# Attention with a gated feed-forward block on one core: the mixed tile's weights and h1 transposed in halves, row sums inverted after they are turned, all jobs in a new order

## The chip, the core and the metric

The kernel runs on one core of a Trainium2 chip. TensorE (PE in the profile) multiplies matrices into PSUM, VectorE (DVE), ScalarE (ACT) and GpSimd (POOL) work on tiles, SyncE (SP) issues most DMAs. The engines run side by side and wait for one another through semaphores; each takes its own instructions in the order in which they were built. The metric is the device time of one execution in microseconds.

## The reference

Queries and keys are rotated (RoPE), softmax attention runs over 8 x 8 heads of 576 positions and 64 dimensions, and the heads of a batch, side by side, feed a gated block of 512 channels. The gate is a causal convolution of five taps. All data are float32.

```python
q_rot, k_rot = rotate(q), rotate(k)                  # 8, 8, 576, 64
scores = q_rot @ k_rot.T / sqrt(64)
attn = exp(scores - max(scores)); attn = attn / (sum(attn) + 1e-9)
x = (attn @ v) with heads side by side               # 8, 576, 512
gate_pre[s] = sum over k < 5 of conv_w[k] * x[s - 4 + k]
gate = 1 / (1 + exp(-gate_pre))
out = (gate * (x @ w_val)) @ w_out
```

## The kernel before

**Pairs.** The 64 heads are worked on as 32 pairs (`p`), two heads on 128 partitions; four pairs make a batch. Loads of k and q are rotated by products with a table and a sum (`rope_mul`, `rope_add`, on GpSimd or VectorE) and split into a high and a low part (`qk_hi`, `qk_lo`).

**Scores.** 576 queries are four chunks of 128 for each head and one *mixed* tile, the last 64 queries of both heads. So a pair has nine tiles of 128 queries by 576 keys. TensorE makes each out of three products of the parts (`s_mm`, L332), VectorE takes the negative maximum (L338), ScalarE the exponential and, beside it, the row sum, into one of nine columns of `sums` (L346).

**Turning the weights.** The product with v needs keys on partitions, so TensorE transposes the exponentials against the identity into PSUM banks (`ps_t`, four of them, tag `ps_t`), and VectorE or ScalarE copies them out (`t_copy`, L427 and L429). A *key* names a group. `"0"` to `"3"` are the chunks; `halves` (L395) turns them with two instructions a block, each on 64 of the 128 rows, into two banks `a` and `b`; `pt0` and `pt1` receive them. 512 of 576 keys lie in these blocks. The last 64 keys of two chunks stand next to each other: `h0` turns those of the two earlier chunks, `h1` of the two later ones, into `ptr`. `m` is the mixed tile, 512 keys in four blocks; `hm` is 73 columns: its last 64 keys and nine columns for the row sums. `h0`, `h1`, `m` and `hm` are full 128-row transposes (`transpose`, L361).

**Row sums.** `r_inv` (L458, L459) adds 1e-9 to `sums` and writes the inverse into the nine columns behind the mixed tile, so that `hm` turns them too. `r_copy` takes the nine rows out of the bank (L472), a DMA writes them to DRAM and another reads them back spread over the partitions (`rb`). `x_norm` (L489) multiplies the product with v (`pv_mm` L438, `pv_left` L448 for the last keys) by `rb`. The last pair does it in another way.

**Gate and block.** x is split in two parts (`x_hi` on ScalarE, `x_lo` on GpSimd), four taps run on VectorE (L515), one and the tanh on ScalarE. After four pairs come the two products of the block, each value out of three products of parts (`f_mm`, L555), with `y_mul` (VectorE), `y_hi` (ScalarE) and `y_lo` (GpSimd) between them. The weights' 64-bit patterns are decoded by steps on VectorE, ScalarE and GpSimd early in the program.

**The order.** The functions only add *jobs* with what they read and write. A table written out by hand, `ORDER`, lists the jobs' numbers; a letter V, A or G behind a number picks the engine where there is a choice, and the digits after a colon pick the buffers (of four `ps_t` banks, two `ps_s`, and so on). `FILLS` names steps ahead of which TensorE turns the identity a number of times into a bank that the next transposition overwrites (L354). So every engine's order is that of the table.

## Time and profile before

| | us |
|---|---|
| median of 3 runs | 709.28 (708.91 to 709.58) |
| profiled execution | 708.45 |
| its span, first to last instruction | 706.6 |
| TensorE busy | 673.5 (95%) |
| VectorE busy | 592.5 (84%) |
| ScalarE busy | 502.7 (71%) |
| GpSimd busy | 298.9 (42%) |
| mean granted clock of TensorE | 0.986 |

A busy time is the union of an engine's instructions. Consecutive matmuls overlap, so the time that one of them costs is read from its start to the start of the next one; the row's own duration is longer. Idle time of an engine counts only where another one waits for it.

### The profile page before, as it was taken

What the parts mean: (1) busy time and instruction counts of PE and PEld (TensorE: products, weight loads), DVE (VectorE), ACT (ScalarE), POOL (GpSimd) and SP (SyncE); (2) the same over time, 40 slices, a digit from 0 to 9 for tenths busy, and PEclk for the clock granted to TensorE, in tenths of its full rate; (3) what the DMA queues carried; (4) which work ended last, traced back from release to release, by engine and by line L of the source; (5) the groups of instructions that cost most, each with busy time, mean ns of one, the idle gap of its engine ahead of it and who ended that gap; (6) DMA issues with size and microseconds to landing.
All of it is one profiled execution on the core that took longest, in us unless ns stands there. A gap on an engine that the chain in (4) does not pass through costs nothing.

```text
span 706.6 us, 17745 instructions
## 1 busy us (share of the span) xinstructions
PE 673.5 (95%) x6988; PEld 539.6 (76%) x6988; DVE 592.5 (84%) x995; ACT 502.7 (71%) x1197; POOL 298.9 (42%) x231
## 2 busy tenths in 40 slices
PE   5888988899999999999999999999999999999998
PEld 4765557668787887877888877777888787888887
DVE  4989998998899888899879988898888888887731
ACT  2677877677978776777788776777777777677622
POOL 2242333556043545463424526536436744542121
PEclk9988998999999999999999999999999999999999
DMA  6343432243442143343432325323233235310212
GB/s 226 96 154 122 119 101 65 82 118 113 137 131 84 36 151 101 94 132 94 151 100 82 112 75 148 120 86 105 88 108 92 63 118 159 102 45 19 69 36 76
DMA packets 47317, 72.63 MB, mean 103 GB/s; under 512 B 15961, under 2 KB 25730, under 8 KB 47234
## 3 DMA queue, kind: packets, MB, share of 16 engines
q1 hardware_dynamic: 46690, 70.91, 32.6%
q8 instruction: 55, 0.90, 0.5%
q10 hardware_dynamic: 544, 0.59, 0.3%
q14 instruction: 28, 0.23, 0.1%
HBM read 61.89 MB, written 9.59 MB: 101 GB/s over the span
## 4 chain that ended last, share of the span: by engine, by line
PE 74%; DVE 14%; ACT 7%; issue 2%; DMA 1%; SPq 1%; POOL 0%; DVEq 0%; ACTq 0%
PE ps_f L555 27%; PE ps_s L332 18%; PE ps_a L438 13%; PE ps_t L395 8%; PE ps_t L361 5%; DVE g L515 4%; DVE nm L338 4%; ACT p L346 3%; PE ps_a L448 3%; ACT pt L427 2%; DVE q L304 1%; PE ps_r L287 1%; DMA rb<-rd 1%; DVE y L563 1%; DVE wst L594 0%
## 5 line engine op out<-in xcount | busy, mean ns | idle before, releaser
L346 ACT ACTIVATE p<-ps_s,nm 128x576 f32<-128x576 f32 x288 | 213.1, 744 | 74.3 <-DVE nm L338 72.8
L338 DVE TENSOR_REDUCE nm<-ps_s 128x1 f32<-128x576 f32 x288 | 207.8, 750 | 41.1 <-PE ps_s L332 36.6
L332 PE MATMUL ps_s<-k,q 64*128 64x288 f32 (+1 forms) x1728 | 180.6, 312 | 11.1 <-ACT p L346 10.6
L332 PEld LDWEIGHTS ps_s<-k,q 64*128 64x128 f32 (+1 forms) x1728 | 141.6, 188 | 40.4 <-ACT p L346 24.6
L427 ACT COPY pt<-ps_t 128x512 f32<-128x512 f32 x205 | 118.1, 590 | 55.3 <-PE ps_t L395 52.7
L438 PE MATMUL ps_a<-pt,v 128*64 128x256 f32 (+1 forms) x1024 | 140.8, 415 | 2.1 <-DVE y L563 1.2
L515 DVE SCALAR_TENSOR_TENSOR g<-x,cw,g 128x576 f32<-128x576 f32 (+1 forms) x132 | 121.4, 922 | 1.4 <-ACT g L512 0.8
L555 PE MATMUL ps_f<-y,wout_hi 128*128 128x288 f32 (+2 forms) x512 | 108.1, 302 | 0.0
L438 PEld LDWEIGHTS ps_a<-pt,v 128*64 128x64 f32 x1024 | 67.4, 137 | 47.8 <-issue 5.5
L395 PEld LDWEIGHTS ps_t<-ident,p 64*128 64x128 f32 x2048 | 83.4, 141 | 24.9 <-issue 7.8
L276 POOL TENSOR_TENSOR kin<-kin,tab 128x576 f32<-128x576 f32 (+1 forms) x33 | 52.5, 1598 | 116.2 <-DMA kin<-in_k 88.4
L395 PE MATMUL ps_t<-ident,p 64*128 64x64 f32 x2048 | 94.6, 228 | 6.2 <-DVE x L489 2.3
L570 POOL TENSOR_TENSOR y<-y,y 128x288 fp32r<-128x288 f32 (+2 forms) x64 | 56.7, 894 | 80.3 <-ACT y L567 76.2
L555 PEld LDWEIGHTS ps_f<-y,wout_hi 128*128 128x128 f32 x512 | 81.7, 188 | 5.8 <-ACT pt L427 2.4
L555 PE MATMUL ps_f<-xh,wval_hi 128*128 128x288 f32 (+2 forms) x256 | 78.2, 308 | 0.2 <-ACT pt L427 0.2
L555 PE MATMUL ps_f<-xl,wval_hi 128*128 128x288 f32 (+2 forms) x256 | 76.1, 299 | 0.0
L555 PE MATMUL ps_f<-xh,wval_lo 128*128 128x288 f32 (+2 forms) x256 | 75.2, 297 | 0.0
L555 PE MATMUL ps_f<-y,wout_lo 128*128 128x288 f32 (+2 forms) x256 | 74.7, 297 | 0.0
L502 POOL TENSOR_TENSOR xl<-x,xh 128x576 fp32r<-128x576 f32 (+2 forms) x33 | 49.0, 1491 | 44.3 <-ACT xh L496 44.3
L276 POOL TENSOR_TENSOR qin<-qin,tab 128x640 f32<-128x640 f32 (+1 forms) x32 | 51.8, 1628 | 37.0 <-DMA qin<-in_q 17.9
L429 DVE COPY pt<-ps_t 128x512 f32<-128x512 f32 x83 | 55.7, 678 | 6.6 <-PE ps_t L395 6.2
L346 ACT ACTIVATION_READ_ACCUMULATOR p<-ps_s,nm 128x1 f32 x288 | 57.6, 200 | 0.0
(87 smaller groups left out, 896.7 us busy)
## 6 DMA issues: line engine op xcount, KB each, us to landing
kin<-in_k SPq DMA_DIRECT2D x31, 576.0 KB, 3.8
qin<-in_q SPq DMA_DIRECT2D x31, 512.0 KB, 3.9
v<-in_v SPq DMA_DIRECT2D x32, 320.0 KB, 3.8
out_t<-o SPq DMA_DIRECT2D x56, 144.0 KB, 2.2
rb<-rd SPq DMA_DIRECT2D x31, 144.0 KB, 3.4
rb<-rd SPq DMA_DIRECT2D x31, 128.0 KB, 3.8
wst<-in_w_val SPq DMA_DIRECT2D x4, 512.0 KB
wst<-in_w_out SPq DMA_DIRECT2D x8, 256.0 KB, 3.1
```

Source lines behind the costliest of these rows:

```text
L276: eng.tensor_tensor(out=t[:, i, a:b], in0=t[:, 0 if p < RAW else i, a:b], in1=table[:, i, a:b], op=ALU.mult)
L332: T.matmul(out=tiles[h][:, half, 0:288], lhsT=st["q"][rows, x, c * 128:c * 128 + 128], rhs=st["k"][rows, y, k0:k0 + 288], start=(i == 0), ...
L338: V.tensor_reduce(out=st[f"nm{i}"], in_=st[f"s{i}"], axis=AX.XY, op=ALU.max, negate=True)
L346: A.activation(out=st[f"p{t}"][:, part].rearrange("p (b x) -> p b x", b=2), in_=st[f"s{i}"], func=AF.Exp, bias=st[f"nm{i}"], scale=1.0, ac ...
L395: T.transpose(out=st["b" + key + x][:, to:to + D], in_=f[rows, at:at + 128], identity=ident[rows, rows])
L427: A.copy(out=dst, in_=src)
L429: V.tensor_copy(out=dst, in_=src)
L438: T.matmul(out=st[f"a{g}"][HEAD[h], 0:n], lhsT=st["v"][:, j, h, :], rhs=st[f"pt{g}"][:, h * 4 + j], start=(j == 0), stop=False)
L502: G.tensor_tensor(out=st["xl"][:, a:b], in0=xs[p % 2][:, 4 + a:4 + b], in1=st["xh"][:, a:b].bitcast(F32), op=ALU.subtract)
L515: V.scalar_tensor_tensor(out=g, in0=x_sb[:, a + k:b + k], scalar=w, in1=g, op0=ALU.mult, op1=ALU.add)
L555: T.matmul(out=acc[:, 0:n], lhsT=wt[w][:, kc, ds], rhs=mv, start=(kc == 0 and i == 0), stop=(kc == NCH - 1 and i == 2))
L570: G.tensor_tensor(out=ffn[b][1][:, dc, lo:hi], in0=ffn[b, "y", dc, lo], in1=ffn[b][0][:, dc, lo:hi].bitcast(F32), op=ALU.subtract)
```

## The change

It has four parts.

1. The mixed tile's four blocks (`m`) and, except for the last pair, the two of `h1` are turned by `halves`, twelve instructions on 64 rows each, into two banks `ma` and `mb`. `h1` has no transposition of its own any more. Each bank is copied out by two jobs: 128x256 into `pt1` and 128x128 into `ptr`; before there was one of 128x512 for `m` and one of 128x256 for `h1`.
2. `r_inv` becomes one GpSimd instruction, which adds 1e-9 and writes the sums behind the mixed tile. The inverse is taken by VectorE in `r_copy`, on the turned 9x128 sums in PSUM, where ScalarE copied. The last pair stays as it was.
3. `ORDER` is a new table, with other choices of engine and of buffers. Counted in the built program, GpSimd has 31 additions of sums and 14 sums and products of the rotation more and four subtractions of k fewer; VectorE has 969 instructions instead of 995 (those it is counted by in the profile), ScalarE sixteen more, without the read-outs of its sums.
4. `FILLS` has 72 transposes of the identity in six places instead of 86 in eight.

```diff
-        if key == "m":
-            srcs = [flat(p, "m")[:, j * 128:(j + 1) * 128] for j in range(4)]
-        elif key == "hm":
+        if key == "hm":
...
     def halves(p, key):
 
         st = state[p]
-        i = order(p).index(int(key))
         for x in "ab":
             if "b" + key + x not in st:
                 st["b" + key + x] = ring("ps_t", [128, 512], F32, "ps_t", psum)
-        for h in range(2):
-            f = flat(p, f"{i // 2}{h}")
-            for j in range(4):
-                at, to = 640 * (i % 2) + j * 128, (h * 4 + j) * D
-                for x, rows in zip("ab", HEAD):
-                    T.transpose(out=st["b" + key + x][:, to:to + D], in_=f[rows, at:at + 128], identity=ident[rows, rows])
+        if key == "m":
+            srcs = [flat(p, "m")[:, j * 128:(j + 1) * 128] for j in range(4)]
+            if p < NP - 1:
+                srcs += [flat(p, f"1{h}")[:, 512:640] for h in range(2)]
+        else:
+            i = order(p).index(int(key))
+            at = 640 * (i % 2)
+            srcs = [flat(p, f"{i // 2}{h}")[:, at + j * 128:at + (j + 1) * 128] for h in range(2) for j in range(4)]
+        for k, src in enumerate(srcs):
+            for x, rows in zip("ab", HEAD):
+                T.transpose(out=st["b" + key + x][:, k * D:(k + 1) * D], in_=src[rows], identity=ident[rows, rows])
...
     def t_copy(p, key, eng):
-        bank = state[p]["b" + key]
-        if key == "m":
-            src = bank.rearrange("p (j h x) -> p j h x", j=4, h=2)
-            dst = turned(p, 1).rearrange("p (h j) x -> p j h x", h=2)[:, :, :, 256:320]
+        both = key[:2] == "h1" and p < NP - 1
+        bank = state[p]["bm" + key[2] if both else "b" + key]
+        if key[0] == "m":
+            x = "ab".index(key[1])
+            src = bank[:, 0:256].rearrange("p (j x) -> p j x", x=D)
+            dst = turned(p, 1)[:, x * 4:x * 4 + 4, 256:320]
+        elif both:
+            at = 128 + "ab".index(key[2]) * D
+            src = bank[:, 256:384].rearrange("p (h x) -> p h x", h=2)
+            dst = turned(p, "r")[:, :, at:at + D]
...
     def r_inv(p, g):
         for a, b in COLS[g]:
             r = sums[p % 2][:, a:b]
-            V.tensor_scalar(out=r, in0=r, scalar1=1e-9, scalar2=None, op0=ALU.add)
-            V.reciprocal(out=r if p == NP - 1 else state[p]["pm"][:, 1, a:b], in_=r)
+            if p == NP - 1:
+                V.tensor_scalar(out=r, in0=r, scalar1=1e-9, scalar2=None, op0=ALU.add)
+                V.reciprocal(out=r, in_=r)
+            else:
+                G.tensor_scalar(out=state[p]["pm"][:, 1, a:b], in0=r, scalar1=1e-9, scalar2=1.0, op0=ALU.add, op1=ALU.mult)
...
-            A.copy(out=st[f"rr{g}"][0:9], in_=st["bhm"][D:D + 9, 0:128])
+            V.reciprocal(out=st[f"rr{g}"][0:9], in_=st["bhm"][D:D + 9, 0:128])
...
-FILLS = {54: (25, 0, '2a', 1), 66: (16, 0, '0a', 2), 82: (11, 0, '3a', 1), 92: (8, 0, '1a', 0), 185: (6, 1, '1a', 3), 362: (8, 3, '1a', 2), 376: (8, 3, 'hm',
-         3), 463: (4, 4, '1a', 3)}
+FILLS = {50: (19, 0, '2a', 1), 63: (14, 0, 'h0', 2), 89: (7, 0, '1a', 3), 282: (9, 2, 'ma', 0), 351: (15, 3, '3a', 2), 377: (8, 3, 'ma', 3)}
```

What the new table does is seen in the built order. TensorE, pair 16, from behind its mixed scores to the next product of the block; before (a chunk's `halves` is the row x16, `h1` the row x2, `hm` the row 73x128, `m` the row x4):

```order
L555 MATMUL ps_f<-y_4300,wout_lo 128x288
L361 MATMUL ps_t<-ident,p 128x128 x2
L395 MATMUL ps_t<-ident,p 128x64 x16
L332 MATMUL ps_s<-k_72,q_74 128x288 x12
L361 MATMUL ps_t<-ident,p 73x128
L361 MATMUL ps_t<-ident,p 128x128 x4
L555 MATMUL ps_f<-xh,wval_hi 128x288
```

The same place now:

```order
L567 MATMUL ps_f<-y_4335,wout_lo 128x288
L398 MATMUL ps_t<-ident,p 128x64 x16
L333 MATMUL ps_s<-k_72,q_74 128x288 x12
L398 MATMUL ps_t<-ident,p 128x64 x12
L362 MATMUL ps_t<-ident,p 73x128
L567 MATMUL ps_f<-xh,wval_hi 128x288
```

The group x2 is gone, `m` and `h1` are the row x12, and `hm` comes after them. Ahead of this place twelve products of the block stand behind the pair's mixed scores, where there were eight.

VectorE before, at the end of the same pair's maxima (the third row is the subtraction of k for the next but one pair, the fourth and fifth are `r_inv`):

```order
L515 SCALAR_TENSOR_TENSOR g<-x_85,cw,g 128x576
L338 TENSOR_REDUCE nm<-ps_s 128x1
L307 TENSOR_TENSOR k_71<-kin,k_71 128x576
L458 TENSOR_SCALAR sums_86<-sums_86 128x9
L459 RECIPROCAL p<-sums_86 128x9
L515 SCALAR_TENSOR_TENSOR g<-x_85,cw,g 128x576
```

GpSimd now, with the same pair's addition of sums among the rotation of later pairs and the low part of an earlier x:

```order
L277 TENSOR_TENSOR qin<-qin,tab 128x640
L281 TENSOR_TENSOR kin<-kin 128x576
L514 TENSOR_TENSOR xl<-x_85,xh 128x576
L471 TENSOR_SCALAR p<-sums_86 128x9
L277 TENSOR_TENSOR kin<-kin,tab 128x576
```

And VectorE now, from the pair's last maximum to the reciprocal of its turned sums:

```order
L339 TENSOR_REDUCE nm<-ps_s 128x1
L308 TENSOR_TENSOR k_71<-kin,k_71 128x576
L527 SCALAR_TENSOR_TENSOR g<-x_85,cw,g 128x576
L438 COPY pt_5398<-ps_t 128x8x64
L527 SCALAR_TENSOR_TENSOR g<-x_85,cw,g 128x576
L339 TENSOR_REDUCE nm<-ps_s 128x1 x2
L484 RECIPROCAL rr<-ps_t 9x128
L575 SCALAR_TENSOR_TENSOR y<-g,ps_f 128x288
```

The two instructions of `r_inv` are gone from VectorE, one is in GpSimd's queue, and the reciprocal stands two maxima of the next pair further on.

280 lines of the change are left out of this document (143 added, 137 removed).

## Prediction

> **What bounds the kernel now.** I read the page's busy times and its 40 slices first. In the second fence the profile is cut into four stretches, whose columns are length, then busy time and instructions of PE, PEld, DVE, ACT and POOL, then granted clock, DMA share and GB/s.
>
> ```profile
> span 706.6 us, 17745 instructions
> PE 673.5 (95%) x6988; PEld 539.6 (76%) x6988; DVE 592.5 (84%) x995; ACT 502.7 (71%) x1197; POOL 298.9 (42%) x231
> PE   5888988899999999999999999999999999999998
> DVE  4989998998899888899879988898888888887731
> PEclk9988998999999999999999999999999999999999
> ```
>
> ```profile
> 0.00:20.00 20.00, 11.52 (x62) 8.63 (x64) 10.30 (x28) 5.90 (x15) 4.35 (x10) 1.00 0.68 221
> 20.00:145.00 125.00, 109.22 (x1092) 79.62 (x1090) 117.84 (x215) 92.81 (x220) 46.55 (x34) 0.92 0.34 104
> 145.00:690.00 545.00, 539.51 (x5745) 438.40 (x5742) 461.58 (x749) 400.06 (x953) 244.59 (x184) 1.00 0.32 99
> 690.00:706.60 16.60, 13.26 (x100) 13.00 (x98) 2.78 (x6) 3.92 (x10) 3.38 (x4) 1.00 0.23 81
> ```
>
> From 145 to 690 TensorE is idle for 5.5 of 545 us while VectorE is idle for 83: what TensorE no longer has to do there shortens the run. From 20 to 145 VectorE is busy for 94% and TensorE for 87%, partly at half clock (0.92 on the mean: 10 us of clock lost). There VectorE is the nearer bound. The first 20 us are loads and the rotation of pair 0, the last 16.6 the tail.
>
> **TensorE, the term that counts most.** Matmuls overlap at their ends, so I take what a group costs from its start to the start of the next. Here is TensorE's timeline (start, us, engine, line, operation), pair 16 in the middle, and three other places where the same groups have other neighbours:
>
> ```profile
> 335.75 0.43 PE L555 MATMUL ps_f<-y,wout_hi 128*128 128x288 f32 x2
> 336.01 0.29 PE L555 MATMUL ps_f<-y,wout_lo 128*128 128x288 f32 x1
> 336.24 0.71 PE L395 MATMUL ps_t<-ident,p 64*128 64x64 f32 x16
> ...
> 327.31 1.07 PE L332 MATMUL ps_s<-k,q 64*128 64x288 f32 x12
> 328.21 0.66 PE L395 MATMUL ps_t<-ident,p 64*128 64x64 f32 x16
> ...
> 361.79 0.38 PE L361 MATMUL ps_t<-ident,p 128*128 128x128 f32 x2
> 362.11 0.71 PE L395 MATMUL ps_t<-ident,p 64*128 64x64 f32 x16
> 362.62 1.10 PE L332 MATMUL ps_s<-k,q 64*128 64x288 f32 x12
> 363.65 0.77 PE L361 MATMUL ps_t<-ident,p 128*73 128x128 f32 x5
> 364.18 0.38 PE L555 MATMUL ps_f<-xh,wval_hi 128*128 128x288 f32 x1
> ...
> 565.28 0.33 PE L361 MATMUL ps_t<-ident,p 128*73 128x128 f32 x1
> 565.37 0.38 PE L555 MATMUL ps_f<-xh,wval_lo 128*128 128x288 f32 x1
> ```
>
> Before: two full transposes (h1) 0.32, sixteen halves 0.51, twelve score matmuls 1.03, five full ones (hm and m) 0.53: 2.39 us. The new order of pair 16 has sixteen halves, twelve scores, twelve halves, and hm alone. Sixteen halves stay 0.51. Scores that are followed by halves take 0.90 (327.31 to 328.21), 0.13 less than before full ones, and that 0.13 is now paid where the twelve halves end. Those cost 12/16 of 0.51, 0.39; hm alone 0.09 (565.28 to 565.37). The last full matmul ahead of halves costs 0.23 (336.01 to 336.24) against 0.13 for one of the two before it (0.26 from 335.75), so 0.10 more. Together 0.51 + 0.90 + 0.39 + 0.13 + 0.09 + 0.10 = 2.12, a gain of 0.27 us a pair. The count over the whole order agrees: 190 full transposes leave at 0.11 (0.53/5), 20.1 us; 380 halves come at 0.032 (0.51/16), 12.2; changes between full and divided array stay (351 and 350): 7.9 us over 32 pairs, 0.25 each. Some 25 pairs are transposed after 145 us: 25 x 0.27 = **6.8 us**. The 14 fills that go (86 to 72) stood in waits and count as nothing; without that cover they are 14 x 0.11 = 1.5 us more.
>
> The Trainium skill speaks against this, in "TensorE: Matmul & The Clock Gate", section "LDWEIGHTS (loading the stationary operand)": a weight load takes its number of columns over 1.2 GHz however few rows it fills. By that, six blocks would go from 6 x 107 = 0.64 us to twelve loads, 1.28. The trace doesn't agree for halves that alternate between the two row halves: sixteen take 0.51 us.
>
> **VectorE, ScalarE and GpSimd.** Prices from the groups by form (busy us, mean ns of one):
>
> ```profile
> L427 ACT COPY pt<-ps_t 128x512 f32<-128x512 f32 x205 | 118.1, 590 | 55.3 <-PE ps_t L395 52.7 <-PE ps_t L361 2.1
> L515 DVE SCALAR_TENSOR_TENSOR g<-x,cw,g 128x576 f32<-128x576 f32 x124 | 116.9, 943 | 0.5
> L429 DVE COPY pt<-ps_t 128x512 f32<-128x512 f32 x83 | 55.7, 678 | 6.6 <-PE ps_t L395 6.2 <-PE ps_t L361 0.3
> L427 ACT COPY pr<-ps_t 128x256 f32<-128x256 f32 x47 | 17.6, 375 | 1.1 <-PE ps_t L361 0.8
> L280 DVE TENSOR_TENSOR kin<-kin 128x576 f32<-128x576 f32 x12 | 11.5, 958 | 0.1
> L472 ACT COPY rr<-ps_t 9x128 f32<-9x128 f32 x31 | 8.0, 259 | 3.1 <-PE ps_t L361 2.4
> L459 DVE RECIPROCAL p<-sums 128x9 f32<-128x9 f32 x31 | 6.7, 216 | 1.1
> L458 DVE TENSOR_SCALAR sums<-sums 128x9 f32<-128x9 f32 x31 | 6.3, 204 | 3.6 <-ACT p L346 3.2
> L429 DVE COPY pr<-ps_t 64x128 f32<-64x128 f32 x13 | 3.6, 275 | 0.2 <-ACT rr L472 0.2
> L276 POOL TENSOR_TENSOR qin<-qin,tab 128x256 f32<-128x256 f32 x2 | 1.4, 724 | 3.1 <-ACT tab L643 3.1
> masks.py:199 POOL TENSOR_SCALAR_AFFINE_SELECT ident<-ident 128x128 f32<-128x128 f32 x1 | 0.3, 292 | 0.1
> ```
>
> Copies out of PSUM: one of 512 columns (0.59 on ScalarE) and one of 256 (0.375) become two of 256 and two of 128; those are bounded by 0.26 (the 128-column row) and 0.375, I take 0.27: 0.97 becomes 1.29 us, +0.32 a pair. Row sums: VectorE loses 0.204 + 0.216, ScalarE loses 0.259; VectorE gains a reciprocal of 9x128 out of PSUM, which no row shows. It lies between 0.216 (9 columns) and 0.678 (512 columns from PSUM); on 9 columns a reciprocal costs 12 ns more than an addition, so I take the 128-column copy, 0.28. Sum for both engines +0.32 - 0.42 - 0.26 + 0.28 = -0.08 a pair: nothing, hidden behind VectorE's 15% and ScalarE's 27% idle time after 145 us. At 0.678 VectorE would carry 31 x 0.4 = 12 us more, 2 of them early. GpSimd's addition on 9 columns lies between 0 and 0.72 (the 256-column row); near the 128-column 0.29, so 0.2.
>
> **VectorE early.** Counted in the built order ahead of the 55th maximum (pair 6's first, near 145 us) VectorE has 242 instructions before and 227 after: six additions and six reciprocals (2.5 us) against five new reciprocals (1.4); two copies of 512 columns and two small ones fewer (1.9); two rotation sums fewer (1.9); one tap fewer (0.9); two small weight steps that leave and one subtraction that comes about cancel. That is 5.8 us less. VectorE is 94% busy there, so I count 85% of it, **4.9 us**. GpSimd takes rotation work over, and with the new additions some 22 us (14 sums and products net, near 1.6 each, less four subtractions, plus 31 x 0.2). What that costs VectorE the next rows show, the first of GpSimd:
>
> ```profile
> 460.53 1.57 POOL L280 TENSOR_TENSOR qin<-qin 128x640 f32<-128x640 f32 x1
> ...
> 460.50 2.21 DVE L515 SCALAR_TENSOR_TENSOR g<-x,cw,g 128x576 f32<-128x576 f32 x1
> ...
> 362.43 0.19 ACT L346 ACTIVATION_READ_ACCUMULATOR p<-ps_s,nm 128x1 f32 x1
> ...
> 362.65 0.17 DVE L458 TENSOR_SCALAR sums<-sums 128x9 f32<-128x9 f32 x1
> 362.86 0.21 DVE L459 RECIPROCAL p<-sums 128x9 f32<-128x9 f32 x1
> 362.99 0.76 DVE L515 SCALAR_TENSOR_TENSOR g<-x,cw,g 128x576 f32<-128x576 f32 x1
> ```
>
> A tap beside a GpSimd sum took 2.21 us, another one 0.76; with the mean at 0.943, 124 taps lose 22 us beside 299 us of GpSimd work, 0.076 per us. 22 us more cost VectorE 1.7 us, mostly hidden. The Trainium skill has a rule for it ("SBUF — State Buffer", section "SBUF: two separate sides": VectorE with two SBUF inputs and GpSimd lock one port pair against each other). The trace agrees, with 2.21 against 0.76.
>
> **The new waits.** hm needs GpSimd's addition, which needs the pair's last exponential, read out at 362.62, when VectorE's addition followed within 0.03 us. In the old order hm starts 1.03 us after that, at 363.65. In the new one twelve full matmuls instead of eight (4 x 0.13) stand ahead of the halves, and from there to hm it is 0.10 + 0.51 + 0.90 + 0.39 + 0.13 = 2.03 instead of 0.32 + 0.51 + 1.03 = 1.86: hm comes 0.7 us later, 1.7 after the exponential. A free GpSimd needs 0.2 to 0.7, so this later place is the cover. If GpSimd has just begun a 1.57 us operation, it is done after 1.8, and behind hm stand all later matmuls of TensorE's order. I take one pair in four as 0.1 late, **+0.8 us**.
>
> The reciprocal of the turned sums moves from ScalarE's queue to VectorE's (in pair 16 behind two maxima), and the write and the read of the row in SP's queue follow it. Two rows say what is waited for now, one of the groups and one of TensorE's waits from 145 to 690 us:
>
> ```profile
> L489 DVE TENSOR_TENSOR x<-ps_a,rb 128x320 f32<-128x320 f32 x32 | 15.4, 483 | 13.3 <-PE ps_a L448 11.1 <-DMA rb<-rd 2.0
> ...
> PE ps_t L361 <- DVE pt L429: 0.4, 1, 0.4
> ```
>
> The row's DMA ended 2.0 us of waits in 32 pairs, TensorE's last matmul 11.1: what comes before it hides a reciprocal that is some tenths later. Without that cover it is 31 x 0.5 = 15 us on VectorE, not on TensorE. The two banks of m and h1 now wait for two copies each instead of one; TensorE waited 0.4 us for such a copy. Both count as nothing.
>
> Sum: -6.8 - 4.9 + 0.8 = -10.9. The profiled execution took 708.45 us (span 706.6 and 1.8 around it); 708.45 - 10.9 = 697.6, and its excess of the median over it, 0.83, gives **698.4 us**.
>
> **Rivals.** (a) The early gain is lost: TensorE's own waits and half clock, not VectorE, set the front. It is 87% busy there with 10 us of clock lost, which speaks for it; VectorE's 94% against it. Only 6.8 - 0.8 remain: 703.3. (b) More is gained: a third of TensorE's 15.8 idle us early closes and a third of the lost clock comes back, 5.3 + 3.4, of which VectorE's 7.2 idle us there allow some 6: 692.4. (c) Slower: GpSimd's addition stands behind an operation of 1.57 us and one tap's use of the port (0.94), so it is done 2.7 us after the exponential and hm comes 1.0 late, in twenty of the 31 pairs: 709.3 - 11.7 + 20 = 717.6. It decides from a mean wait of 0.38 us at hm (11.7/31). For it: GpSimd is 45% busy after 145 us and works in order. Against it: it is idle for the other 55%, and what stands ahead of the addition is work for later pairs. (d) No change: the same wait near 0.38, 709.3.
>
> **How the numbers follow.** The likeliest is the forecast, 0.57, with a range of its own of 694 to 702.5; (a) 0.18; (b) 0.14; (c) 0.07; (d) 0.04. The range 690.5 to 705 holds the forecast, (a) and most of (b). Under 0.2% (1.4 us) can't be told from no change here: faster 0.89, same 0.04, slower 0.07.
>
> **What would show it.** Right: full transposes down to hm and h0; the stretch after 145 us equal in idle time to before and shorter by 7 us; VectorE near 578 us; the maximum that stood at 145 us reached some 5 us earlier. Wrong: waits of TensorE for GpSimd's addition above 2 us in total, taps above 0.943 us on the mean, a reciprocal near 0.7, more half-clock time, or the front's end unmoved.

## The result, and the profile after

The changed kernel takes **729.27 us** (median of 6 runs, 726.74 to 731.54), the kernel before 709.43 beside it: a ratio of **1.0264**, 95% interval 1.0230 to 1.0297. It is 2.6% slower where 1.5% faster was forecast, and lies above the range. The profiled execution took 726.74 us.

The page of the changed kernel, busy times and slices:

```profile
span 725.0 us, 18171 instructions
PE 673.5 (93%) x7164; PEld 540.3 (75%) x7164; DVE 608.9 (84%) x969; ACT 499.3 (69%) x1213; POOL 330.5 (46%) x273
PE   5788787989999999999999999999999999999998
DVE  4899899999988889898889988889879889978641
PEclk9977799999999999999999999999999999999999
```

Its four stretches (length, then busy time and instructions of PE, PEld, DVE, ACT and POOL, granted clock, DMA share, GB/s):

```profile
0.00:20.00 20.00, 11.00 (x75) 8.44 (x76) 9.81 (x27) 6.01 (x15) 4.57 (x10) 1.00 0.59 188
20.00:145.00 125.00, 104.82 (x1057) 77.86 (x1056) 117.30 (x195) 87.57 (x216) 51.85 (x40) 0.88 0.35 109
145.00:690.00 545.00, 526.17 (x5804) 424.84 (x5803) 471.25 (x727) 397.80 (x964) 266.85 (x214) 1.00 0.32 98
690.00:725.00 35.00, 31.54 (x234) 29.17 (x232) 10.59 (x22) 7.90 (x20) 7.22 (x9) 1.00 0.17 60
```

VectorE should have come to about 578 us and stands at 608.9. TensorE's busy time is the same 673.5 us, but after 145 us it is idle for 18.8 of 545 us where it was 5.5. The early stretch has more half clock (0.88 against 0.92), not less. The groups of the changed kernel say what grew:

```profile
L527 DVE SCALAR_TENSOR_TENSOR g<-x,cw,g 128x576 f32<-128x576 f32 x124 | 119.4, 963 | 1.0 <-ACT g L524 0.4
...
L484 DVE RECIPROCAL rr<-ps_t 9x128 f32<-9x128 f32 x31 | 29.5, 952 | 2.5 <-ACT pr L436 1.3 <-PE ps_t L362 0.4
...
L471 POOL TENSOR_SCALAR p<-sums 128x9 f32<-128x9 f32 x31 | 11.3, 363 | 83.1 <-ACT p L347 78.1 <-PE ps_f L567 4.5
```

The new reciprocal takes **0.952 us**, where 0.28 was counted and 0.678 was the upper bound. Its 29.5 us, less the 6.3 and 6.7 of the old addition and reciprocal, are 16.5: as much as VectorE's busy time grew by (592.5 to 608.9); its other gains and losses (rotation, copies, taps) about cancel. The taps' mean rose by 0.020 us, 2.5 in sum. And this is how it looks on VectorE's timeline (start, us, engine, line, operation; in brackets the idle time before and what ended it) when the reciprocal stands between the two maxima of a chunk, with one row of ScalarE behind it:

```profile
537.03 0.69 DVE L438 COPY pt<-ps_t 128x512 f32<-128x512 f32 x1 [0.46 <-PE ps_t L398]
537.85 0.76 DVE L339 TENSOR_REDUCE nm<-ps_s 128x1 f32<-128x576 f32 x1
538.66 0.95 DVE L484 RECIPROCAL rr<-ps_t 9x128 f32<-9x128 f32 x1
539.64 0.76 DVE L339 TENSOR_REDUCE nm<-ps_s 128x1 f32<-128x576 f32 x1
540.32 1.89 DVE L305 SCALAR_TENSOR_TENSOR q<-qin,q 128x640 fp32r<-128x640 f32 x1
...
539.65 0.42 ACT L436 COPY pr<-ps_t 64x128 f32<-64x128 f32 x2 [0.83 <-DVE rr L484]
```

The second maximum comes 1.0 us later. ScalarE is held up too: it waits 0.83 us for the reciprocal, and behind its copies stand the exponentials of both maxima. Directly, though, the others wait little for the reciprocal: in the whole trace ScalarE 2.4 us, TensorE 3.5, GpSimd 1.6. TensorE's longest waits over the whole span, the first also for the kernel before (us in total, times, longest):

```profile
PE ps_s L333 <- ACT p L347: 18.4, 27, 1.8
PE ps_r L288 <- POOL kin L277: 8.8, 1, 8.8
```

```profile
PE ps_s L332 <- ACT p L346: 10.6, 20, 1.5
```

The one for the exponentials grew by 7.8 us; the other stands at the start of the program, and was 7.5. The start of each maximum against the same one before shows when the time is lost: the first comes 0.5 us later, the 37th 7.0, the 55th 3.1 (5 earlier was forecast), the 181st 7.4, the 217th 12.6, the last of the 288 comes 18.8 later.

### The profile page after: what moved, and what is told of

The parts are those of the page before. It is cut to its first block, busy times and chain, and to the rows that moved or that the text cites. A ratio compares the mean times of both kernels' runs of the same rounds, so it can differ in the third digit from the quotient of the medians.

```text
span 725.0 us, 18171 instructions
## 1 busy us (share of the span) xinstructions
PE 673.5 (93%) x7164; PEld 540.3 (75%) x7164; DVE 608.9 (84%) x969; ACT 499.3 (69%) x1213; POOL 330.5 (46%) x273
## 4 chain that ended last, share of the span: by engine, by line
PE 44%; DVE 9%; ACT 2%; issue 2%; ACTq 0%; DVEq 0%
PE ps_f L567 18%; PE ps_s L333 10%; PE ps_a L447 8%; PE ps_t L398 6%; DVE nm L339 3%; DVE g L527 2%; PE ps_a L457 2%; DVE rr L484 1%; ACT p L347 1%; PE ps_t L362 1%; DVE q L305 1%; DVE pt L438 0%; ACT pt L436 0%; DVE y L575 0%; ACT q L297 0%
## 5 line engine op out<-in xcount | busy, mean ns | idle before, releaser
L333 PE MATMUL ps_s<-k,q 64*128 64x288 f32 (+1 forms) x1728 | 185.1, 314 | 19.2 <-ACT p L347 18.4
L333 PEld LDWEIGHTS ps_s<-k,q 64*128 64x128 f32 (+1 forms) x1728 | 144.4, 190 | 51.8 <-ACT p L347 38.5
L436 ACT COPY pt<-ps_t 128x512 f32<-128x512 f32 (+1 forms) x236 | 125.1, 548 | 55.8 <-PE ps_t L398 55.5
L447 PE MATMUL ps_a<-pt,v 128*64 128x320 f32 (+1 forms) x1024 | 140.2, 416 | 3.8 <-ACT pt L436 1.1
L398 PE MATMUL ps_t<-ident,p 64*128 64x64 f32 x2428 | 118.3, 230 | 9.7 <-DVE pt L438 2.7
L398 PEld LDWEIGHTS ps_t<-ident,p 64*128 64x128 f32 x2428 | 103.9, 142 | 28.8 <-issue 7.1
L527 DVE SCALAR_TENSOR_TENSOR g<-x,cw,g 128x576 f32<-128x576 f32 (+2 forms) x132 | 124.1, 942 | 1.3 <-ACT g L524 0.7
L447 PEld LDWEIGHTS ps_a<-pt,v 128*64 128x64 f32 x1024 | 69.1, 138 | 49.7 <-issue 5.1
L277 POOL TENSOR_TENSOR qin<-qin,tab 128x640 f32<-128x640 f32 (+1 forms) x40 | 66.6, 1677 | 41.1 <-DMA qin<-in_q 34.7
L277 POOL TENSOR_TENSOR kin<-kin,tab 128x576 f32<-128x576 f32 (+1 forms) x31 | 51.5, 1666 | 50.6 <-DMA kin<-in_k 43.1
L438 DVE COPY pt<-ps_t 128x512 f32<-128x512 f32 (+1 forms) x84 | 51.4, 618 | 5.1 <-PE ps_t L398 4.6
```

Of the source, the lines that this page charges most:

```text
L277: eng.tensor_tensor(out=t[:, i, a:b], in0=t[:, 0 if p < RAW else i, a:b], in1=table[:, i, a:b], op=ALU.mult)
L333: T.matmul(out=tiles[h][:, half, 0:288], lhsT=st["q"][rows, x, c * 128:c * 128 + 128], rhs=st["k"][rows, y, k0:k0 + 288], start=(i == 0), ...
L398: T.transpose(out=st["b" + key + x][:, k * D:(k + 1) * D], in_=src[rows], identity=ident[rows, rows])
L436: A.copy(out=dst, in_=src)
L438: V.tensor_copy(out=dst, in_=src)
L447: T.matmul(out=st[f"a{g}"][HEAD[h], 0:n], lhsT=st["v"][:, j, h, :], rhs=st[f"pt{g}"][:, h * 4 + j], start=(j == 0), stop=False)
```

## The experiments

Each run is given as its ratio to the kernel before on the same chip, with the 95% interval; 0.1% is 0.7 us. Theory R is that the long reciprocal is the loss; O, that the new order is; G, that GpSimd's additions are. Some runs undo the change in parts, others edit the kernel before to find out what sets its time.

### A copy in the reciprocal's place

```diff
-            V.reciprocal(out=st[f"rr{g}"][0:9], in_=st["bhm"][D:D + 9, 0:128])
+            V.tensor_copy(out=st[f"rr{g}"][0:9], in_=st["bhm"][D:D + 9, 0:128])
```

> The changed kernel, with VectorE's reciprocal of the turned sums (0.95 us each in the trace) made a plain copy on VectorE (near 0.28): the inverse is left out, all else stays. Theory R (the reciprocal on 128 columns costs VectorE some 0.67 us a pair more than was counted, 21 us in all, and TensorE's waits follow from it): 698 to 706 us, TensorE idle near 35 us. Rival O (the new order itself, with GpSimd held by the additions and more half clock): 720 to 729, VectorE 20 us less busy, TensorE's waits unchanged.

711.24 us, ratio 1.0041 (1.0022 to 1.0059). Its busy times, and the row that took the reciprocal's place:

```profile
PE 669.7 (94%) x7164; PEld 538.7 (76%) x7164; DVE 588.4 (83%) x969; ACT 499.1 (70%) x1213; POOL 325.2 (46%) x273
...
L484 DVE COPY rr<-ps_t 9x128 f32<-9x128 f32 x31 | 8.8, 285 | 3.4 <-ACT pr L436 2.2 <-PE ps_t L362 0.5
```

VectorE's busy time falls by 20.5 us and the time by 2.2% (1.0264 to 1.0041), 16 us. So the reciprocal is most of the loss, although the time stays above theory R's 698 to 706 us. And with the price that the prediction had put on it (0.285 against 0.28) the change is still 0.4% slower than the kernel before, not 1.5% faster: a second error of some 14 us lies elsewhere. The profiles say where. The copy's run reaches the 55th maximum 2.2 us later than the kernel before, where 4.9 earlier was forecast; from there to the end it takes 562.6 us against 561.9, where 6.0 less was forecast. So each of the two main terms missed by some 7 us. VectorE's busy time, too, is 10 us above the 578 that were forecast.

### The sums as before, in the new order; the new sums, in the old order; the new order alone

In the first, `r_inv` and `r_copy` are those of the kernel before, at the new table's places:

```diff
-                G.tensor_scalar(out=state[p]["pm"][:, 1, a:b], in0=r, scalar1=1e-9, scalar2=1.0, op0=ALU.add, op1=ALU.mult)
+                V.tensor_scalar(out=r, in0=r, scalar1=1e-9, scalar2=None, op0=ALU.add)
+                V.reciprocal(out=state[p]["pm"][:, 1, a:b], in_=r)
...
-            V.reciprocal(out=st[f"rr{g}"][0:9], in_=st["bhm"][D:D + 9, 0:128])
+            A.copy(out=st[f"rr{g}"][0:9], in_=st["bhm"][D:D + 9, 0:128])
```

> The changed kernel with its second part undone: VectorE adds and inverts nine columns (0.20 + 0.22 us) and ScalarE copies the turned sums, each at the place that the new order gives the job. R: 698 to 706, about as the kernel with the copy. O: 720 to 729. Rival G (the addition in GpSimd's queue holds up the rotation behind it): clearly under the kernel with the copy, by 5 us or more.

724.81 us, ratio 1.0214 (1.0181 to 1.0248): in theory O's range, and rival G fails. The second is the opposite edit in the kernel before:

```diff
-            V.tensor_scalar(out=r, in0=r, scalar1=1e-9, scalar2=None, op0=ALU.add)
-            V.reciprocal(out=r if p == NP - 1 else state[p]["pm"][:, 1, a:b], in_=r)
+            if p == NP - 1:
+                V.tensor_scalar(out=r, in0=r, scalar1=1e-9, scalar2=None, op0=ALU.add)
+                V.reciprocal(out=r, in_=r)
+            else:
+                G.tensor_scalar(out=state[p]["pm"][:, 1, a:b], in0=r, scalar1=1e-9, scalar2=1.0, op0=ALU.add, op1=ALU.mult)
...
-            A.copy(out=st[f"rr{g}"][0:9], in_=st["bhm"][D:D + 9, 0:128])
+            V.reciprocal(out=st[f"rr{g}"][0:9], in_=st["bhm"][D:D + 9, 0:128])
```

> The kernel before with the second part alone: GpSimd adds, VectorE inverts the turned sums on 128 columns; order and transposes as before. R: VectorE carries 31 x (0.95 - 0.42) = 16 us more, most of it early or ahead of maxima: 716 to 728. O: 707 to 712.

731.96 us, ratio 1.0317 (1.0283 to 1.0350), and on its page:

```profile
PE 678.0 (93%) x6988; PEld 538.2 (74%) x6988; DVE 617.0 (84%) x964; ACT 494.4 (68%) x1166; POOL 312.9 (43%) x262
```

The new sums alone cost 3.2%, more than the whole change; VectorE's busy time is 24.5 us longer (16.5 by the reciprocal less what it replaces, the rest by other rows), the time 22.5. That is beyond theory R's range, and O's 707 to 712 fails. The third is the kernel before with `ORDER` as the new table has it. Where that has two copies for `ma` and `mb` (or `h1a` and `h1b`) the earlier place gets the one copy of `m` (or `h1`).

```diff
 ORDER = """
-...
+...
-FILLS = {54: (25, 0, '2a', 1), 66: (16, 0, '0a', 2), 82: (11, 0, '3a', 1), 92: (8, 0, '1a', 0), 185: (6, 1, '1a', 3), 362: (8, 3, '1a', 2), 376: (8, 3, 'hm',
-         3), 463: (4, 4, '1a', 3)}
+FILLS = {50: (19, 0, '2a', 1), 63: (14, 0, 'h0', 2), 89: (7, 0, '1a', 3), 280: (9, 2, 'm', 0), 348: (15, 3, '3a', 2), 374: (8, 3, 'm', 3)}
```

> The new order with the old transposes (m and h1 in full, at the places of the new halves, copied whole at the first of their copies' places) and the old row sums. R: the order itself is no loss, TensorE carries the 8 to 13 us of full transposes again: 706 to 715. O: 728 to 740.

722.93 us, ratio 1.0199 (1.0168 to 1.0229), between the two theories. So the new order costs 2% with full transposes and 2.1% with halves, when the sums are the old ones: at equal order the halves bring nothing that can be measured. With the new sums, though, the new order and the halves are 0.5% better than the old order (1.0264 against 1.0317, with intervals that just overlap). Its places are chosen for these sums. What this run and the one with the old sums measure is the order with jobs that it wasn't made for, and I take the copy's run as the fairer test of it. That run shows what the reciprocal costs at its place. It doesn't show that the new order would do well with any other sums: with the old ones it loses 2.1% without a 9x128 reciprocal.

### What a reciprocal costs

Behind the last instruction of the kernel before, reciprocals and other instructions of several sizes, three of each:

```diff
+        for n in (2, 9, 32, 64, 128, 256, 512):
+            for _ in range(3):
+                V.reciprocal(out=two[:, 0:n], in_=one[:, 0:n])
+        for n in (9, 128):
+            for _ in range(3):
+                V.reciprocal(out=two[0:9, 0:n], in_=one[0:9, 0:n])
+                V.reciprocal(out=two[0:9, 0:n], in_=bank[0:9, 0:n])
...
```

> The kernel before, with 57 VectorE instructions after its last one: reciprocals of 2, 9, 32, 64, 128, 256 and 512 columns on 128 partitions, three each, and of 9 and 128 columns on 9 partitions and from PSUM, beside copies, additions and products of the same sizes. Theory P (an element of a reciprocal costs VectorE about 7.4 ns whatever the partitions and the memory): 128 columns 0.95 us on 9 and on 128 partitions, from SBUF and PSUM alike, 512 columns 3.8 us, 9 columns 0.21 us; copies of 128 columns 0.2 to 0.3 us. Rival Q (the 0.952 us comes from PSUM, or from the few partitions): 128 columns of 128 partitions from SBUF below 0.5 us.

The time of this one execution (747.76 us) isn't used, only its rows (`probe` is the PSUM bank):

```profile
L809 DVE RECIPROCAL x<-x 128x512 f32<-128x512 f32 x3 | 10.1, 3353 | 0.1
...
L809 DVE RECIPROCAL x<-x 128x128 f32<-128x128 f32 x3 | 2.9, 953 | 0.1
L813 DVE RECIPROCAL x<-probe 9x128 f32<-9x128 f32 x3 | 2.8, 946 | 0.1
L812 DVE RECIPROCAL x<-x 9x128 f32<-9x128 f32 x3 | 2.8, 941 | 0.1
...
L817 DVE TENSOR_TENSOR x<-x 128x128 f32<-128x128 f32 x3 | 0.9, 292 | 0.1
...
L809 DVE RECIPROCAL x<-x 128x9 f32<-128x9 f32 x3 | 0.6, 216 | 0.1
...
L817 DVE TENSOR_TENSOR x<-x 128x9 f32<-128x9 f32 x3 | 0.5, 170 | 0.1
```

A column of a reciprocal costs (3353 - 216) / 503 = 6.2 ns, one of a product (292 - 170) / 119 = 1.0 ns. The price of a reciprocal is the same for 9 and 128 partitions and for both memories. So turning the sums from 128x9 to 9x128 makes the same 1152 inverses 0.74 us dearer. Theory P holds; only its 7.4 ns a column contained the fixed part. The Trainium skill ("VectorE: DVE Perf Modes", section "First, the fixed hardware budget") says that the reciprocal runs on iterative-divide operations with a repeat count of 8. The trace agrees that it is dear: a column costs six times as much as one of a product.

### No addition, in the old and in the new order

A row sum holds the exponential of its own maximum, about 1, so adding 1e-9 in float32 leaves it as it is. In the kernel before the addition is left out:

```diff
-            V.tensor_scalar(out=r, in0=r, scalar1=1e-9, scalar2=None, op0=ALU.add)
             V.reciprocal(out=r if p == NP - 1 else state[p]["pm"][:, 1, a:b], in_=r)
```

> The kernel before, with one thing left out: the addition of 1e-9 to the row sums. (A row sum holds the exponential of its own maximum, about 1, so in fp32 the sum stays as it is.) VectorE's 31 rows of a 128x9 addition, 5 to 6 us, go; nothing else changes. The four runs so far lie near a line in VectorE's work within one order: in the old order 650.7 us of VectorE gave 708, 672.1 us gave 732, so 1.1 us of time for each us of VectorE's work. Theory R (VectorE's work sets the time within an order): 702 to 704 us, ratio 0.991 to 0.994. Rival S (the price is the waiting at one place, where the long reciprocal stands, and a little less work elsewhere brings nothing): 707 to 709 us, within 0.2%.

706.23 us, ratio **0.9954** (0.9929 to 0.9979): the one version that is faster than both kernels beyond its interval. It lies between the two theories: only half of the expected gain came, and VectorE's busy time on its page is 592.0 us, hardly less than 592.5, although 6.3 us of additions are gone. The same group in the kernel before and in this one:

```profile
L304 DVE SCALAR_TENSOR_TENSOR q<-qin,q 128x640 fp32r<-128x640 f32 x31 | 30.4, 980 | 0.7 <-ACT q L296 0.5
```

```profile
L304 DVE SCALAR_TENSOR_TENSOR q<-qin,q 128x640 fp32r<-128x640 f32 x31 | 34.4, 1111 | 0.5 <-ACT q L296 0.5
```

In this profile 4.0 us of the gain went into the subtractions of q, each 0.13 us longer. That needn't come from the missing addition: the same 31 rows took 1.097 us on the mean in the run with more transposes below, and 1.061 in the one with the prices, which both have the addition. The new order and the halves with the same sums:

```diff
-                G.tensor_scalar(out=state[p]["pm"][:, 1, a:b], in0=r, scalar1=1e-9, scalar2=1.0, op0=ALU.add, op1=ALU.mult)
+                V.reciprocal(out=state[p]["pm"][:, 1, a:b], in_=r)
...
-            V.reciprocal(out=st[f"rr{g}"][0:9], in_=st["bhm"][D:D + 9, 0:128])
+            A.copy(out=st[f"rr{g}"][0:9], in_=st["bhm"][D:D + 9, 0:128])
```

> The changed kernel (new order, halves) with the sums inverted before they are turned, as 128x9 on VectorE (0.216 us by the kernel before), copied by ScalarE once turned, and without the addition of 1e-9; GpSimd is held up by nothing of this. The same work on the sums as in the old order without the addition, beside it in this call: the two differ by the order and the halves alone. Theory O (the new order with its halves is itself slower at equal work of VectorE, by what the line through the new order's four runs gives: 643.8 us of VectorE 711, 664.6 us 729): VectorE about 652, 716 to 719 us, 13 to 16 us above the old order without the addition. Rival R alone (only VectorE's work counts): no more than 4 us above it, 703 to 709 us.

716.56 us, ratio 1.0080 (1.0057 to 1.0104): 10.3 us above the old order with the same sums and within 1.3 us of the same VectorE busy time (593.3), within theory O's 716 to 719. And with VectorE as the one that copies the turned sums, since that place was VectorE's:

```diff
-            A.copy(out=st[f"rr{g}"][0:9], in_=st["bhm"][D:D + 9, 0:128])
+            V.tensor_copy(out=st[f"rr{g}"][0:9], in_=st["bhm"][D:D + 9, 0:128])
```

> New order and halves, the sums inverted as 128x9 on VectorE without the addition, as in the run of 716.6 us, but the turned sums copied by VectorE (0.285 us) where there ScalarE did it (0.259 us): the new order's place for this job was chosen for VectorE. There the exponential's waits at the hand-over were 51.0 us in 127 rounds, with the copy on VectorE and a GpSimd addition they were 43.1. Theory S (ScalarE's copy at a place that was not its own cost the difference): 711 to 714 us. Rival V (VectorE's work counts, 31 x 0.285 = 8.8 us more of it): 719 to 725 us.

714.95 us, ratio 1.0096 (1.0066 to 1.0127): beyond theory S's range, and no different from ScalarE's copy by these intervals. So 31 copies more on VectorE, 8.8 us, cost little or nothing at this place, where ScalarE lost 8.0 us of copies: rival V fails, and not everything that VectorE gains is paid in time.

### More fills; the old engines

The copy's kernel with 66 fills in the first pair instead of 40 (the inverse is left out here too; the kernel before has 60 there and 6 in the second pair):

```diff
-FILLS = {50: (19, 0, '2a', 1), 63: (14, 0, 'h0', 2), 89: (7, 0, '1a', 3), 282: (9, 2, 'ma', 0), 351: (15, 3, '3a', 2), 377: (8, 3, 'ma', 3)}
+FILLS = {50: (25, 0, '2a', 1), 63: (22, 0, 'h0', 2), 89: (19, 0, '1a', 3), 282: (9, 2, 'ma', 0), 351: (15, 3, '3a', 2), 377: (8, 3, 'ma', 3)}
```

> The changed kernel with a copy in the place of the 9x128 reciprocal (the inverse left out), which took 711.2 us and had 31 us of half clock, 27 of them before 125 us, where the kernel before has 20.5; and 26 more of the transposes that only keep TensorE at work in the first pair, so that it has 66 there, as many as the kernel before. Theory C (the rest of the loss is TensorE's clock, from the fewer fills): half clock falls to about 20 us, and the time to 704 to 707 us. Rival F (the front's loss is in how the new order queues VectorE's and GpSimd's work there, and the clock follows from TensorE's waiting): the fills change the time by less than 2 us, 709.5 to 713 us, whatever becomes of the clock.

710.41 us, ratio 1.0006 (0.9985 to 1.0027), 0.35% below the copy's run with intervals that just overlap, and no longer told apart from the kernel before. Early half clock (the stretches in which the trace has the granted clock at 0.5) goes from 30.7 to 27.3 us only, so theory C's condition, 20 us, isn't met, and its 704 to 707 us didn't come; a small gain by the fills isn't excluded. The other run keeps the new places but gives the 97 rope, subtraction and weight steps that had changed engine their old one, with sums as in the run of 716.56 us:

```diff
 ORDER = """
-... 13G ... 32V ...
+... 13V ... 32G ...
```

> The changed order and halves with the sums as in the run without the addition (inverted as 128x9 on VectorE, copied by ScalarE), which took 716.6 us; and for each rope, subtraction and weight step that may go to GpSimd or to VectorE, the engine that the kernel before gave it, at the new order's place. In the new order GpSimd does 14 more of these, and VectorE's 132 convolution taps took 130.9 us, against 121.7 in the old order, so that VectorE's sum is the same although it has fewer instructions. Theory G (the extra work on GpSimd slows VectorE's taps, and this is what the new order costs): taps back at 122 us, 707 to 712 us. Rival H (the places were chosen for the engines, and what the new order costs lies in where its copies and taps stand): 716 us or more.

724.16 us, ratio 1.0214 (1.0184 to 1.0243). Theory G fails, rival H holds; the taps stay slow (129.5 us in 132 of them, 130.9 with the new engines).

### What sets the time of the kernel before

Two heads' score tiles fill the two `ps_s` buffers in rounds: score matmuls, two maxima, the second exponential, the next score matmuls. First, 128 copies of 128x1 on ScalarE stand in that chain, ahead of every second exponential; then the same copies one place later, behind it:

```diff
+        bias = st[f"nm{i}"]
+        if i % 2:
+            bias = link[i // 2 % 2]
+            A.copy(out=bias, in_=st[f"nm{i}"])
```

> The kernel before, with one more ScalarE instruction for each odd score tile (128 of them): a copy of its 128x1 negated maximum to another place, and the exponential takes its bias from there, so that the copy stands between maximum and exponential. By the traces so far the two score tiles' PSUM banks go round in one chain: score matmuls, two maxima, the second exponential, the next score matmuls. After the first six pairs this chain is 511.5 of the 518.8 us in the kernel before (127 rounds of 4.03 us: 1.10 matmuls, 1.43 maxima, 0.74 exponential, and waits of 0.24, 0.31 and 0.21 at the three hand-overs). Theory T (this rotation sets the time): a link of some 0.2 us (a ScalarE read of an accumulator of 128x1 takes 0.19) makes each of 128 rounds longer, less where TensorE is late anyway: 15 to 28 us more, 724 to 737 us. Rival W (only each engine's sum of work counts, and ScalarE at 71% is no bound): 0 to 4 us more, 709 to 713 us.

```diff
+        if i % 2:
+            A.copy(out=link[i // 2 % 2], in_=st[f"nm{i}"])
```

> The same 128 copies on ScalarE, each one place later: behind the exponential, which takes its bias from the maximum itself, as in the kernel before. Theory T: ScalarE's queue is longer by the same 26 us, but the rotation isn't, apart from rounds whose next step finds ScalarE busy: 0 to 8 us more, 709 to 717 us, well under the run with the link in the chain. Rival W2 (it is ScalarE's work itself that costs, wherever it stands): as much as with the link in the chain.

In the chain: 716.37 us, ratio 1.0101 (1.0085 to 1.0118). Beside it: 707.89 us, ratio 0.9990 (0.9967 to 1.0012). The row of the first:

```profile
L350 ACT COPY link<-nm 128x1 f32<-128x1 f32 x128 | 24.4, 191 | 27.0 <-DVE nm L339 26.1 <-ACT p L351 0.2
```

Its 24.4 us cost 7 in the chain and nothing beside it. The place counts, which is theory T's mechanism, but less than half of its price came: some two thirds vanish in the chain too. Then TensorE gets more to do, three more transposes of the identity in each of 31 pairs:

```diff
+        if key == "hm" and p < NP - 1:
+            for j in (1, 2, 3):
+                T.transpose(out=bank[:, j * 128:(j + 1) * 128], in_=ident, identity=ident)
```

> The kernel before, with three more transposes of the identity in each of 31 pairs, behind the one that turns the mixed tile's last columns and in the same bank: 93 transposes at 0.11 us are 10 us more for TensorE, the opposite of what the halves save. Theory T (TensorE's work counts only where TensorE is the late one in the rotation, 0.21 us of a round of 4.03): 1 to 5 us more, 710 to 715 us. Rival B (as the prediction counted: after the front a us of TensorE's work is a us of time): 8 to 11 us more, 717 to 721 us.

715.24 us, ratio 1.0095 (1.0061 to 1.0129), between the two theories. 93 transposes, 10 us at the prediction's 0.11, cost 6.7, by the interval 4.3 to 9.1. In this run's trace the stretch from hm to the next group is 0.27 us longer (median of 25 pairs), 8.4 us for 31 pairs. So more work for TensorE does count, for most of its length and perhaps for all.

### The maxima together

Last, one edit in both orders: where another VectorE instruction stands between the two maxima of a round, the second maximum is moved ahead of it; 29 places in the kernel before without the addition, 36 in the changed kernel. One of these places (830 is the reciprocal of pair 7, 951 and 953 are the two maxima):

```diff
-818:01 ... 819A 820V 821:30 951:0 828:1 521 829A 830:1 952:2 953:3 522
+819A 820V 821:30 951:0 953:3 828:1 521 829A 830:1 952:2 522
```

> The kernel before without the addition of 1e-9 (706.2 us), and in 29 places where another VectorE instruction stands between the two maxima of a round (after the first six pairs 28 instructions, 20 us) the second maximum is moved ahead of it. The interval from the first maximum's start to the second's end is 181.3 us in 127 rounds of that kernel, where 2 x 0.745 us would make 172. Theory T+B (rotation and TensorE's stream are both close to the end: the link in the rotation cost 7.8 us of the 24 that it took, the rest came out of TensorE's lateness, and 93 more transposes cost 6.6 us): the rotation's 9 us mostly turn into lateness of TensorE, 702 to 706 us. Rival T alone: all 9 us, 696 to 699 us. Rival N: the copies and taps that are moved back are then late for ScalarE and TensorE: 707 us or more.

> The changed kernel, whole, with the same edit in 36 places (in 8 pairs after the sixth the reciprocal of 0.952 us stands between two maxima; that interval is 191.8 us in 127 rounds, against 181.6 before). Theory Q (the place of the reciprocal is a part of the loss, a third or so; its work in VectorE's queue ahead of the next maximum is the rest): 718 to 724 us against 729. Rival P (its place there is the loss): 709 to 715 us. Rival V (VectorE's sum alone counts): within 2 us of the changed kernel, 727 to 731 us.

In the old order 708.83 us, ratio 1.0015 (0.9995 to 1.0035), where the kernel without the edit had 0.9954: it costs 0.6% (rival N). In the changed kernel 728.79 us, ratio 1.0307 (1.0275 to 1.0340): no gain. The same pair's reciprocal as on the timeline of the changed kernel above (the 25th of 31), in this run:

```profile
539.31 1.42 DVE L339 TENSOR_REDUCE nm<-ps_s 128x1 f32<-128x576 f32 x2
540.76 0.95 DVE L484 RECIPROCAL rr<-ps_t 9x128 f32<-9x128 f32 x1
```

The reciprocal is out of the round and the time stays. Rival P, that its place there is the loss, fails; rival V's range holds. But the edit moves copies and taps too, and that cost 0.6% in the old order, so a gain of a few us by the reciprocal's new place could be hidden: theory Q, a third of the loss, isn't excluded.

### Two tables over the runs

The first adds up the rounds after the sixth pair, 127 of them, from the starts and ends of their rows: from the first score matmul to the end of the last, to the first maximum, through both maxima, to the second exponential, and from its end to the next round's first matmul (us in sum; a round of the mixed tile has one maximum and one exponential; the last column holds the exponentials too, 94.1 to 94.5 in each run).

| run | matmuls | to maximum | maxima | to exponential | to matmuls | sum |
|---|---|---|---|---|---|---|
| before | 139.0 | 29.8 | 181.6 | 39.8 | 26.8 | 511.5 |
| link in the chain | 143.2 | 28.7 | 181.4 | 63.6 | 6.6 | 517.5 |
| more transposes | 140.0 | 33.5 | 181.2 | 41.0 | 31.4 | 521.3 |
| no addition | 139.9 | 32.2 | 181.3 | 41.2 | 25.4 | 514.4 |
| no addition, maxima together | 137.7 | 27.7 | 163.7 | 53.0 | 38.5 | 515.0 |
| old order, new sums | 145.2 | 48.0 | 189.7 | 36.2 | 23.2 | 536.6 |
| after | 143.1 | 35.4 | 191.8 | 44.5 | 15.6 | 524.8 |
| after, a copy for the reciprocal | 142.6 | 29.0 | 187.1 | 43.1 | 14.1 | 510.3 |
| after, maxima together | 140.2 | 33.2 | 163.7 | 61.1 | 32.3 | 524.9 |

The second sets VectorE's busy time, from each page, against the span of the same execution; the ratio is that of all executions. One profile can lie some us off its kernel's median: that of "VectorE copies" is the fastest of its six executions, 3.8 us below it.

| run | VectorE busy | span | idle | ratio |
|---|---|---|---|---|
| no addition, maxima together | 586.0 | 708.9 | 122.9 | 1.0015 |
| no addition | 592.0 | 704.6 | 112.6 | 0.9954 |
| before | 592.5 | 706.6 | 114.1 | 1 |
| link in the chain | 593.2 | 713.7 | 120.5 | 1.0101 |
| same copies beside the chain | 592.0 | 706.9 | 114.9 | 0.9990 |
| more transposes | 595.9 | 714.6 | 118.7 | 1.0095 |
| old order, new sums | 617.0 | 731.6 | 114.6 | 1.0317 |
| after, copy, more fills | 587.7 | 707.8 | 120.1 | 1.0006 |
| after, copy | 588.4 | 709.5 | 121.1 | 1.0041 |
| new order, no addition | 593.3 | 716.9 | 123.6 | 1.0080 |
| new order alone | 595.2 | 720.2 | 125.0 | 1.0199 |
| new order, no addition, VectorE copies | 597.2 | 709.4 | 112.2 | 1.0096 |
| new order, no addition, old engines | 598.7 | 724.9 | 126.2 | 1.0214 |
| new order, old sums | 601.5 | 723.6 | 122.1 | 1.0214 |
| after, maxima together | 608.3 | 726.5 | 118.2 | 1.0307 |
| after | 608.9 | 725.0 | 116.1 | 1.0264 |

## Why the prediction was wrong, point by point

**The reciprocal (the first step that failed).** "It lies between 0.216 (9 columns) and 0.678 (512 columns from PSUM); on 9 columns a reciprocal costs 12 ns more than an addition, so I take the 128-column copy, 0.28." It took 0.952. So the sum for both engines, "nothing", was some 21 us short for VectorE (31 x 0.67). The upper bound was the price of another operation, and the comparison was made at nine columns, where the fixed part of some 0.15 us hides the price of a column. The profile of the kernel before had the better row, among the last pair's groups:

```profile
L459 DVE RECIPROCAL p<-sums 128x9 f32<-128x9 f32 x31 | 6.7, 216 | 1.1
...
L459 DVE RECIPROCAL sums<-sums 128x2 f32<-128x2 f32 x3 | 0.5, 166 | 0.1
```

Seven columns more cost 50 ns, 7.1 ns each: 216 + 119 x 7.1 gives 1.06 us for 128 columns. The run with a copy shows what the error cost, 16 us of the 31 between forecast and result.

**"hidden behind VectorE's 15% and ScalarE's 27% idle time after 145 us".** For the reciprocal this cover didn't hold. From before to the old order with the new sums VectorE's busy time grows by 24.5 us and the span by 25.0; from the copy's run to the changed kernel it is 20.5 and 15.5. In every run of the second table VectorE is idle for 112 to 126 us, at 586 to 617 us busy. Its longest wait in the kernel before (us in total, times, longest):

```profile
DVE nm L338 <- PE ps_s L332: 36.6, 62, 1.8
```

It is idle there because the next scores don't exist yet. That a longer queue makes these scores late by as much is my reading; it fits these runs, and none tests it alone. The additions say the same, more or less by the order: between the two runs of the new order that differ by VectorE's additions of 1e-9 alone (8.3 us in 31 pairs) the ratio goes from 1.0080 to 1.0214, in the old order (6.3 us) from 0.9954 to 1. It isn't a rule for all work: the 31 copies of 0.285 us were nearly free, and the new order alone takes 2.0% longer at 595.2 us busy, against 592.5. "At 0.678 VectorE would carry 31 x 0.4 = 12 us more" should have been a term of the sum, or a rival at least.

**TensorE, -6.8 us.** The groups themselves came out as priced. In the changed kernel, around the reciprocal shown above:

```profile
536.26 0.71 PE L398 MATMUL ps_t<-ident,p 64*128 64x64 f32 x16
...
536.77 1.11 PE L333 MATMUL ps_s<-k,q 64*128 64x288 f32 x12
...
537.65 0.71 PE L398 MATMUL ps_t<-ident,p 64*128 64x64 f32 x12
...
538.29 0.33 PE L362 MATMUL ps_t<-ident,p 128*73 128x128 f32 x1
...
538.38 0.38 PE L567 MATMUL ps_f<-xh,wval_hi 128*128 128x288 f32 x1
```

From 536.26 to 538.38 it is 2.12 us, where 0.51 + 0.90 + 0.39 + 0.13 + 0.09 = 2.02 were counted and 2.39 stood before; over all groups of twelve halves that wait for nothing the next group starts after 0.53 us (median of 21), where 0.39 + 0.13 were counted. The step that failed is the first one: "what TensorE no longer has to do there shortens the run". With the same order and sums the halves brought nothing (1.0214 with them, 1.0199 without). TensorE's rows fill 99% of the time after 145 us, but the time doesn't hang on all of them: in the first table TensorE is late for 26.8 us of the rounds, and the link in the chain could take 20 of these. The copy's run did gain 12.7 us of this lateness (26.8 to 14.1) and lost as much elsewhere: the matmuls are 3.6 longer, the interval of the maxima 5.5, the wait for ScalarE 3.3. I read this as TensorE arriving earlier at hand-overs where VectorE or ScalarE isn't ready. But the halves also bring more copies, and which of the two took the gain no run separates.

**VectorE early, -4.9 us.** The 55th maximum came 3.1 us later, and 2.2 later with a copy for the reciprocal, so this term was lost for another reason than the reciprocal, as in rival (a), and worse. Four other profiles of the old order (the prices, the link, the copies beside it, the transposes) have this maximum from 2.4 us earlier to 0.4 later, so 2 us are within what differs between profiles; the distance from 4.9 earlier isn't. The stretch from 20 to 30 us in the kernel before:

```profile
20.00:30.00 10.00, 8.93 (x116) 7.94 (x112) 9.86 (x16) 5.10 (x13) 4.42 (x3) 1.00 0.18 54
```

and in the changed one:

```profile
20.00:30.00 10.00, 6.88 (x77) 5.53 (x76) 10.00 (x15) 5.93 (x14) 6.61 (x4) 0.95 0.24 87
```

VectorE is full in both, TensorE does less and GpSimd more. Early half clock is 30.7 us instead of 20.5; in the copy's run the first 30 rounds have 2.6 us longer score matmuls and 4.0 us more of waiting for VectorE than in the kernel before. With more fills these are 0.9 shorter and 1.0 longer than in the kernel before, and the 55th maximum stands where it stood there, still not 4.9 us earlier; with the old engines it comes 4.5 us later. Instructions counted ahead of a place say what VectorE must do until then, not when its inputs come. Which of the moved jobs makes the early rounds late stays open.

**Copies, "nothing".** The sum of both engines' copies of turned weights grew by 7 us (207.1 to 214.0, both engines' groups into `pt` and `pr`, as the profile names `pt0`, `pt1` and `ptr`), near the 10 us that were priced (31 x 0.32). In the new order with the old sums the taps are slower with the halves too (128.6 us, 123.1 without, 116.9 in the kernel before). These two may be what ate the halves' gain; it is argued from the rows, not tried.

**The new wait at hm, +0.8 us, and rival (c).** As a wait of TensorE it was next to nothing. This is what the trace of the changed kernel says of GpSimd's addition (idle ahead of it by releaser: us, times; then who waited for it):

```profile
  ACT p L347: 78.1, 25
...
  PEld ps_t L362: 0.4, 1
```

GpSimd waits for the exponentials, 78 us in all, and TensorE waited for this addition once. The addition cost 0.363 on the mean, not 0.2, within the bounds. Nor did it help to free GpSimd of it: without the addition, and VectorE inverting 128x9 instead (6.4 us), the new order stood at 1.0096, the copy's run with it at 1.0041.

**Taps, 1.7 us.** 2.5 us in the changed kernel: right in size.

**The rivals.** None had more work on VectorE in it. (a) has the early gain lost, which happened; that TensorE's waits and clock are the reason isn't shown. (c), the slower one, named GpSimd's addition. Of the signs of being wrong, four came: a reciprocal above 0.7, taps above 0.943, more half clock, and the front's end, not earlier but 3.1 us later; the waits for GpSimd's addition stayed far below 2 us.

**What stays open** is why the new order with the halves is slower than the old one at about equal busy time of VectorE: by 0.4% in the copy's run, by nothing that can be told with more fills, by 1.3% between the two runs without the addition. In the profiles of these two, 6.4 of the 12.2 us between them stand at the 55th maximum, so about half of it is lost in the early rounds. Without GpSimd's additions, with another engine for the turned sums' copy, or with the maxima together it wasn't gone; with the rope's old engines it was worse, at places that were chosen for the new ones. How much the halves' own copies have of it, no run separates.

## What to carry to other kernels

Price an operation by its slope over two sizes of the same operation, not by another operation of the same size; a reciprocal belongs on the layout with the fewest columns, here 128x9 and not 9x128. Idle time of an engine that hands work round in a ring may be no cover, as for the reciprocal here: before work is put there, ask for what the engine is waiting, and whether its own delay would make that wait longer. Where two engines are both nearly late, a gain of one can end at the other; the time between hand-overs, added up over the rounds, shows how late each one is (here TensorE 26.8 us of 511.5).

## What the hardware showed that I had not expected

A reciprocal costs VectorE 6.2 ns a column, six times a product (1.0 ns), on 9 partitions as on 128 and from PSUM as from SBUF (0.941 to 0.958 us for 128 columns). GpSimd's small addition costs 0.2 to 0.83 us from one instance to another. And the mean of a group that no edit touched can differ by a tenth between profiles: the 31 subtractions of q took 0.980 to 1.097 us in runs of the old order that keep the additions, and 1.111 in the one without them, where VectorE's busy time stayed nearly where it was though 6.3 us of work were gone.
